# The first two chunks of z in another tile, TensorE's first waits filled; first expert tile's rows in the diagonal's tile, second list in smaller pieces

## Chip, cores and metric

One core of one Trainium2 chip. The metric is the device time of the whole kernel in microseconds (us); the kernel before has a median of 2366.27 us over 3 runs.

## What is computed

Eight batches of an attention without softmax, whose result is gated by u, and then a mixture of eight experts in which each token goes to its best one:

```python
scores = (1.0 / S) * np.matmul(z, z.transpose(0, 2, 1))      # z: 8 x 2496 x 64
out = np.matmul(np.maximum(scores, 0.0) ** 2, v)              # v: 8 x 2496 x 256
x = (u * out).reshape(B * S, D)                               # 19968 tokens of 256
logits = x @ w_gate                                           # 8 experts
expert_idx, gate_w = argmax(logits), softmax(logits) at that place
for e in range(8):                                            # w1: 256 x 1024, w2: 1024 x 256
    out[tokens of e] = gate_w * (np.maximum(x[tokens of e] @ w1[e], 0.0) @ w2[e])
```

All of it is fp32. TensorE gets each fp32 operand as two parts, a rounded high one and the low rest, and adds three products.

## The kernel before

**Attention.** A batch has five query chunks (four of 512, the last of 448) and ten pairs of key blocks for each: 400 steps in all, in the list `steps`. A step has `scores` (matmuls L292 and L293, ReLU and square on ScalarE, the high part L303 and the low part L305 on VectorE, or tiles that an earlier chunk has stored and that are turned back, L265 to L267) and `weighted` (matmuls L329 to L332 into the two `acc` banks). Scores are made three steps ahead (`LA`). The scores of a chunk with itself are kept in the tile `sd`, from which L298 mirrors one half.

**z and v.** `fetch_z` and `fetch_v` issue DMAs on SyncE's queue (SP), `split_z` (L117 to L123) and `split_v` (L133, L135) make the two parts. In the first batch the low part of v and the high part of the later z chunks are made on GpSimd (POOL). The tile `zr` has 2 buffers, `vr` 2.

**Routing.** After a chunk, `gate_x` makes x, `turn_rows` turns it into token rows by DMA transposes (L372), `logits` (L382 to L391) computes the logits and turns them into the tile `lg`, and `route` (choose from L420 on, exps, place) finds the expert and the place of each token, writes the rows to `xrows` in DRAM (L462, L464) and the token numbers to the list `lst` (L467). These pieces lie in a queue, `bg`, from which one is taken per step; `nothing` fills a turn.

**Experts.** `tile_list` makes a list of expert tiles. List "A" is made before the last batch ends and has six tiles of 512 tokens; list "F" needs all tokens and is made while list A's tiles run. A tile's rows are gathered (`load_x`, L681, 4 gathers on POOL into a tile `rows`, which has 3 buffers), turned (`turn_x`, L712, 4 DMA transposes on SP into `th`, of which there are 3), and the gate column is copied (L714, on VectorE, into `gt`); `split_x` (L724 to L727) makes the two parts of x. Then come 8 groups per tile: `up` (L744, 12 matmuls into a bank `ph`, L748 on ScalarE and L749 on VectorE) and `down` (L765, L767), two groups behind (`LU`). `ph` and `acc` share a ring of three PSUM banks. `finish` multiplies by the gate (L777) and scatters the rows out (L779). The weights of a tile are fetched by `load_w` (L672) and split by `split_piece` (L701 to L704).

**Order.** The Tile scheduler orders the instructions of each engine by a model of the time; each engine then runs its own in that order, and waits at the first that can't start. What is `pinned` is issued behind the last instruction so far of each engine. The table `loads` says at how many steps from the last one the first expert tile's weights and rows are fetched:

```python
    loads = {NKP + 4: [lambda: load_w(0, 0), lambda: load_w(0, 1)],
             NKP + 3: [lambda: load_x(0)],
             NKP - 1: [lambda: load_w(1, 0)],
             NKP - 4: [lambda: load_x(1)],
             NKP - 5: [lambda: turn_x(0)],
             1: [lambda: load_x(2)],
             0: [lambda: turn_x(1)]}
```

## Time and profile before

| | us |
|---|---|
| median of 3 runs (lowest, highest) | 2366.27 (2364.37, 2368.11) |
| the profiled execution | 2356.92 |
| its span | 2355.2 |
| TensorE busy | 2303.9 (98%) |
| VectorE busy | 1649.2 (70%) |
| ScalarE busy | 1423.5 (60%) |
| GpSimd busy | 641.6 (27%) |
| mean granted TensorE clock | 0.991 |

The span is what the trace covers; the profiled execution is 1.7 us longer and lies 9.35 us under the median. All times of the trace are counted from the span's start. The attention ends and the experts begin between 1365 and 1430 us; list A's tiles run first, the others follow to 2345 us.

### The profile page before, as it was taken

What the parts mean: (1) busy time and instruction counts of PE and PEld (TensorE: products, weight loads), DVE (VectorE), ACT (ScalarE), POOL (GpSimd) and SP (SyncE); (2) the same over time, 40 slices, a digit from 0 to 9 for tenths busy, and PEclk for the clock granted to TensorE, in tenths of its full rate; (3) what the DMA queues carried; (4) which work ended last, traced back from release to release, by engine and by line L of the source; (5) the groups of instructions that cost most, each with busy time, mean ns of one, the idle gap of its engine ahead of it and who ended that gap; (6) DMA issues with size and microseconds to landing.
All of it is one profiled execution on the core that took longest, in us unless ns stands there. A gap on an engine that the chain in (4) does not pass through costs nothing. (4 is left out here: it accounts for less than half of the span.)

```text
span 2355.2 us, 32513 instructions
## 1 busy us (share of the span) xinstructions
PE 2303.9 (98%) x11636; PEld 1937.7 (82%) x11636; DVE 1649.2 (70%) x3078; ACT 1423.5 (60%) x1944; POOL 641.6 (27%) x639
## 2 busy tenths in 40 slices
PE   8999999999999999999999988999999999999998
PEld 6888887888888888887888876788888888888887
DVE  8868868868868868868868846655666557557554
ACT  6757648658658648648658644355555556556443
POOL 4111111111111111111111225345445445346322
PEclk9999999999999999999999999999999999999999
DMA  5636637747647547547546767465657647557620
GB/s 136 102 65 120 114 62 121 109 68 133 103 69 139 88 78 135 91 74 131 98 75 115 126 114 130 115 150 166 170 140 193 148 133 198 149 147 190 148 87 28
DMA packets 424921, 280.16 MB, mean 119 GB/s; under 512 B 358380, under 2 KB 381690, under 8 KB 415536
## 3 DMA queue, kind: packets, MB, share of 16 engines
q1 hardware_dynamic: 393360, 158.91, 38.7%
q0 software_dynamic: 31392, 119.10, 18.5%
q8 instruction: 93, 1.52, 0.3%
q14 instruction: 76, 0.62, 0.1%
HBM read 149.79 MB, written 43.43 MB: 82 GB/s over the span
## 5 line engine op out<-in xcount | busy, mean ns | idle before, releaser
L332 PE MATMUL acc<-thi,t 128*128 128x512 f32 (+1 forms) x1600 | 619.9, 388 | 0.0
L329 PE MATMUL acc<-thi,t 128*128 128x512 f32 (+1 forms) x1600 | 595.7, 391 | 5.8 <-DVE thi L303 5.6
L331 PE MATMUL acc<-tlo,t 128*128 128x512 f32 (+1 forms) x1520 | 590.7, 389 | 4.3 <-DVE tlo L305 3.4
L765 PE MATMUL y<-t,t 128*128 128x512 f32 x1062 | 384.7, 399 | 4.5 <-ACT t L748 4.5
L749 DVE SCALAR_TENSOR_TENSOR t<-ph,t 128x512 fp32r<-128x512 f32 (+1 forms) x328 | 221.1, 675 | 235.0 <-ACT t L748 232.6
L744 PE MATMUL ph<-thi,t 128*128 128x512 f32 (+2 forms) x1248 | 379.9, 362 | 0.9 <-ACT thi L726 0.9
L467 POOL DMA_INDIRECT lst<-toks,posi x160 | 190.8, 1193 | 640.7 <-DVE posi L459 573.2
L748 ACT ACTIVATE t<-ph 128x512 fp32r<-128x512 f32 (+1 forms) x328 | 192.0, 588 | 279.6 <-PE ph L744 274.8
L329 PEld LDWEIGHTS acc<-thi,t 128*128 128x128 f32 x1600 | 300.9, 189 | 60.1 <-DVE thi L303 6.8
L332 PEld LDWEIGHTS acc<-thi,t 128*128 128x128 f32 x1600 | 301.8, 189 | 55.6
L331 PEld LDWEIGHTS acc<-tlo,t 128*128 128x128 f32 x1520 | 287.1, 189 | 58.7 <-DVE tlo L305 7.2
L767 PE MATMUL y<-t,t 128*128 128x256 f32 x1062 | 297.0, 283 | 10.8 <-DVE t L749 10.8
L744 PEld LDWEIGHTS ph<-thi,t 128*128 128x128 f32 x1248 | 227.3, 190 | 39.5 <-ACT thi L726 1.3
L765 PEld LDWEIGHTS y<-t,t 128*128 128x128 f32 x1062 | 200.8, 189 | 49.0 <-ACT t L748 4.9
L744 PE MATMUL ph<-tlo,t 128*128 128x512 f32 (+2 forms) x624 | 225.9, 362 | 0.8 <-DVE tlo L727 0.8
L767 PEld LDWEIGHTS y<-t,t 128*128 128x128 f32 x1062 | 202.3, 190 | 21.6 <-DVE t L749 12.6
L779 POOL DMA_INDIRECT out_dram<-tf,lfidx x136 | 143.3, 1054 | 276.5 <-DVE tf L777 246.6
L293 PE MATMUL ps_s<-t,t 128*128 128x512 f32 (+1 forms) x480 | 179.0, 377 | 0.0
L301 ACT ACTIVATE tf<-ps_s 128x1024 f32<-128x1024 f32 (+2 forms) x129 | 116.8, 906 | 92.2 <-PE ps_s L293 45.5
L681 POOL DMA_INDIRECT rows<-xrows,lfidx x136 | 141.3, 1039 | 44.1 <-issue 39.2
L303 DVE CAST thi<-tf 128x1024 fp32r<-128x1024 f32 (+2 forms) x129 | 85.1, 660 | 82.8 <-ACT tf L302 78.4
L267 DVE TENSOR_TENSOR tlo<-ps_s,thi 128x896 fp32r<-128x896 f32 (+1 forms) x80 | 89.1, 1114 | 61.4 <-ACT thi L266 60.9
(250 smaller groups left out, 3999.9 us busy)
## 6 DMA issues: line engine op xcount, KB each, us to landing
vr<-in_v_dram SPq DMA_DIRECT2D x80, 256.0 KB, 2.9
xrows<-rows SPq DMA_DIRECT2D x32, 544.0 KB, 3.9
u<-in_ut_dram SPq DMA_DIRECT2D x32, 512.0 KB, 4.5
zr<-in_zt_dram SPq DMA_DIRECT2D x40, 256.0 KB, 5.0
u<-in_ut_dram SPq DMA_DIRECT2D x8, 448.0 KB, 5.4
xrows<-rows SPq DMA_DIRECT2D x8, 408.0 KB, 3.6
rows<-th SPq DMA_TRANSPOSE x160, 4.7
lst<-toks,posi POOLq DMA_INDIRECT x160
```

The costliest lines, as they stand in the source:

```text
L293: nc.tensor.matmul(ps[:, i, m:n], lhsT=hl_k, rhs=lh_q[:, m:n], start=False, stop=True)
L329: nc.tensor.matmul(acc[d][:, :n], lhsT=vh, rhs=hi[:, i, :n], start=first and i == 0, stop=False)
L331: nc.tensor.matmul(acc[d][:, :n], lhsT=vh, rhs=lo[:, i, :n], start=False, stop=False)
L332: nc.tensor.matmul(acc[d][:, :n], lhsT=vl, rhs=hi[:, i, :n], start=False, stop=last and i == 1)
L467: i = nc.gpsimd.indirect_dma_start(out=lst1, out_offset=bass.IndirectOffsetOnAxis(ap=posi[:m, j:j + 1], axis=0), in_=toks[:m, col + j:col ...
L681: nc.gpsimd.indirect_dma_start(out=xg[:, s, :], out_offset=None, in_=src, in_offset=bass.IndirectOffsetOnAxis(ap=lists[which]["idx"][:, s, ...
L744: nc.tensor.matmul(o, lhsT=w1[:, part, dd, fs], rhs=xx[:, dd, :n], start=p == 0, stop=p == 5)
L748: nc.scalar.activation(hh[:, :m], ph[:, :m], AF.Relu)
L749: nc.vector.scalar_tensor_tensor(hl[:, :m], ph[:, :m], 0.0, hh[:, :m].bitcast(F32), op0=ALU.max, op1=ALU.subtract)
L765: nc.tensor.matmul(y, lhsT=hh[:, cs], rhs=w2[:, f % 2].rearrange("p i d -> p (i d)"), start=f == 0, stop=False)
L767: nc.tensor.matmul(y[:, 0:D], lhsT=hl[:, cs], rhs=w2[:, f % 2, 0, :], start=False, stop=f == NF - 1)
L779: d = nc.gpsimd.indirect_dma_start(out=out, out_offset=bass.IndirectOffsetOnAxis(ap=lists[which]["idx"][:, s, t:t + 1], axis=0), in_=yo[:, ...
```

## The change

At the start the first two chunks of z go into the tile `x` instead of the `zr` ring, so that the third one is fetched with them and each later one a step earlier; the low parts of the first two pieces of v are made on VectorE instead of GpSimd; and 4 and 8 warm-up matmuls on zeros are pinned behind the scores of step 0 and of step 1.

At the change from attention to experts the rows of the first expert tile are gathered into the tile `sd` (which gets the size of `rows`); `load_x`, `turn_x` and the gate copy (now `take_gates`, apart from `turn_x`) have new places in the table, and the functions in it are pinned. The last chunk's routing has four empty turns in `bg` instead of two. The second list is cut into 15 pieces instead of 9, and the weights of list F's first expert are fetched only after tile 3 has begun.

```diff
     def fetch_z(b, c):
         w = P * 4
-        zraw[b, c] = sb.tile([P, w], F32, name="zr", tag="zr", bufs=2)
+        if b == 0 and c < 2:
+            if c == 0:
+                zfirst.append(sb.tile([P, 2, QC], F32, name="x", tag="x"))
+            zraw[b, c] = zfirst[0][:, c]
+        else:
+            zraw[b, c] = sb.tile([P, w], F32, name="zr", tag="zr", bufs=2)
...
-        eng = nc.gpsimd if b == 0 else nc.vector
+        eng = nc.gpsimd if b == 0 and kp > 1 else nc.vector
...
+    fetch_z(0, 2)
     split_z(0, 0)
...
-        bg.extend([nothing] * 2 + route(b * S + q0, n, ns, lg, xr))
+        bg.extend([nothing] * (4 if b == B - 1 and c == NC_ - 1 else 2) + route(b * S + q0, n, ns, lg, xr))
...
-        return r, [count] + ([middle, others] if ns else []) + [experts, rows, nothing, nothing, lambda: places(0), lambda: places(1)]
+        return r, [count, middle, middle2, lambda: others([(0, nd, 2 * BS, ndbl)]),
+                   lambda: others([(1, nb, BS, nbig)]), remaining, lambda: experts(parts[:2]),
+                   lambda: experts(parts[2:]), experts2, rows, rows2, nothing, nothing,
+                   lambda: places(0), lambda: places(1)]
...
-        xg = ring_rows()
+        xg = ring_sd() if i == 0 else ring_rows()
...
-        gates[i] = sb.tile([P, BS], F32, name="gt", bufs=4)
-        nc.vector.tensor_copy(gates[i][:, 0:k], xgs.pop(i)[:, 0:k, D].bitcast(F32))
-        turned[i] = tp
+        turned[i] = tp
+
+    def take_gates(i):
+        gates[i] = sb.tile([P, BS], F32, name="gt", bufs=4)
+        nc.vector.tensor_copy(gates[i][:, 0:blocks[i]], xgs.pop(i)[:, 0:blocks[i], D].bitcast(F32))
...
+    pinned(lambda: warm_up(4))
     ready[1] = scores(*steps[1])
+    pinned(lambda: warm_up(8))
...
-             NKP + 3: [lambda: load_x(0)],
-             NKP - 1: [lambda: load_w(1, 0)],
-             NKP - 4: [lambda: load_x(1)],
-             NKP - 5: [lambda: turn_x(0)],
-             1: [lambda: load_x(2)],
-             0: [lambda: turn_x(1)]}
+             NKP + 2: [lambda: load_x(0)],
+             NKP + 1: [lambda: load_x(1)],
+             NKP - 1: [lambda: load_w(1, 0), lambda: turn_x(0)],
+             NKP - 3: [lambda: take_gates(0)],
+             NKP - 4: [lambda: load_x(2)],
+             NKP - 5: [lambda: turn_x(1)],
+             NKP - 7: [lambda: take_gates(1)]}
...
-            if kp % 2 == 0 and kp // 2 + 2 < NC_:
-                fetch_z(0, kp // 2 + 2)
+            if kp % 2 == 0 and kp // 2 + 3 < NC_:
+                fetch_z(0, kp // 2 + 3)
...
-                for w, h in ((wof[i] + 1, 1), (wof[i] + 2, 0)):
-                    if own[i] and w <= wof[hi - 1]:
+                for w, h in ((wof[i] + 1, 0), (wof[i] + 1, 1), (wof[i] + 2, 0)):
+                    if own[i] and w <= wof[hi - 1] and (w, h) not in weights and (w < NA or i > NA):
                         load_w(w, h)
...
             if i + 2 < hi and g == G // 2:
                 turn_x(i + 2)
+                take_gates(i + 2)
```

How the order of the instructions changes, at three places. VectorE at the start; L121 to L123 are the z split before (L130 to L132 now), L303 and L305 the parts of the scores (L318 and L320 now), L144 is the low part of v, L209 to L216 the constants:

```order
L121 CAST t_238<-zr 64x512
L123 TENSOR_TENSOR t_237<-zr,t_238 64x512
L121 CAST t_315<-zr 64x512
L303 CAST thi<-tf 128x1024
L122 TENSOR_TENSOR t_238<-zr,t_237 64x512
```

```order
L144 TENSOR_TENSOR t_196<-vr,t_196 128x512
L212 CAST e_down<-sd 128x8
L209 CAST wg_105<-wg_sb 128x2x8
...
L130 CAST t_251<-zr 64x512
L130 CAST t_328<-zr 64x512
L215 MEMSET x 1x272
L216 MEMSET x 128x256
L210 TENSOR_TENSOR wg_105<-wg_sb,wg_105 128x2x8
L131 TENSOR_TENSOR t_251<-zr,t_250 64x512
L213 COPY base<-base_121 128x8
L318 CAST thi<-tf 128x1024
```

The first high part of the scores now stands behind both low parts of v, most of the constants and a part of the splits of the third and fourth chunk of z.

VectorE at the end of attention; L714 is the gate copy before (L753 now), L267 the low part of a turned tile (L281 now), L702 and L704 weights (L738 and L740 now), L762 and L765 the split of x:

```order
L704 TENSOR_TENSOR t_13524<-s_13124,t_13524 128x2x256
L714 COPY gt<-rows 128x4
L702 TENSOR_TENSOR t_13552<-s_13124,t_13552 128x512
L267 TENSOR_TENSOR tlo<-ps_s,thi 128x2x448
L388 COPY lp<-lt 16x512
```

```order
L740 TENSOR_TENSOR t_13547<-s_13135,t_13547 128x2x256
L738 TENSOR_TENSOR t_13570<-s_13135,t_13570 128x512
L281 TENSOR_TENSOR tlo<-ps_s,thi 128x2x448
L753 COPY gt<-sd 128x4
L403 COPY lp<-lt 16x512
L404 COPY lp<-lt 16x512
L281 TENSOR_TENSOR tlo<-ps_s,thi 128x2x448
L383 COPY th<-x 128x1024
L740 TENSOR_TENSOR t_13571<-s_13135,t_13571 128x2x256
L762 COPY x<-th 128x1024
```

The gate copy now stands behind the low part on which the scores of the last chunk wait, and the split of the first expert tile three rows behind the next one.

SP from the rows of the fourth chunk on; L712 is `turn_x` before (L748 now), L391 the logits' transposes (L406 now), L372 the rows' (L387 now), L462 and L464 the writes of `xrows` (L477 and L479 now):

```order
L462 DMA xrows<-rows 128x4x272
L141 DMA u<-in_ut_dram 128x2x448
L712 DMA_TRANSPOSE th<-rows 128x4x128
L391 DMA_TRANSPOSE lg<-lp 128x4x16 x2
L372 DMA_TRANSPOSE rows<-th 128x4x128 x4
L712 DMA_TRANSPOSE th<-rows 128x4x128 x7
L462 DMA xrows<-rows 128x4x272
L712 DMA_TRANSPOSE th<-rows 128x4x128 x7
L391 DMA_TRANSPOSE lg<-lp 128x4x16 x2
L372 DMA_TRANSPOSE rows<-th 128x4x128 x4
L712 DMA_TRANSPOSE th<-rows 128x4x128
L462 DMA xrows<-rows 128x3x272
```

```order
L477 DMA xrows<-rows 128x4x272
L748 DMA_TRANSPOSE th<-sd 128x4x128 x4
L150 DMA u<-in_ut_dram 128x2x448
L406 DMA_TRANSPOSE lg<-lp 128x4x16 x2
L387 DMA_TRANSPOSE rows<-th 128x4x128 x4
L748 DMA_TRANSPOSE th<-rows 128x4x128 x4
L477 DMA xrows<-rows 128x4x272
L748 DMA_TRANSPOSE th<-rows 128x4x128 x5
L406 DMA_TRANSPOSE lg<-lp 128x4x16 x2
L387 DMA_TRANSPOSE rows<-th 128x4x128 x4
L748 DMA_TRANSPOSE th<-rows 128x4x128 x11
L477 DMA xrows<-rows 128x3x272
```

All four transposes of the first tile now come ahead of u and of the fourth chunk's logits. Ahead of the last chunk's logits stood 15 transposes of tiles 0 to 3, and stand 13 (tiles 0 to 2 and one of tile 3); the last chunk's rows come before the rest of tile 3.

## Rows read from the trace of the kernel before

**Rows 1.** The page: busy time of each engine, share of the span, instructions

```profile
PE 2303.9 (98%) x11636; PEld 1937.7 (82%) x11636; DVE 1649.2 (70%) x3078; ACT 1423.5 (60%) x1944; POOL 641.6 (27%) x639
```

**Rows 2.** Waits of TensorE, whole run: line, released by: us, times, longest

```profile
PE y L767 <- DVE t L749: 10.8, 4, 5.4
PE ps_s L292 <- DVE tlo L267: 6.9, 1, 6.9
PE acc L329 <- DVE thi L303: 5.6, 2, 4.5
PE y L765 <- ACT t L748: 4.5, 1, 4.5
PE acc L331 <- DVE tlo L305: 3.4, 3, 2.2
PE ps_s L292 <- DVE t L123: 2.3, 1, 2.3
```

**Rows 3.** Windows: stretch, us; busy of each engine; granted clock, DMA share, GB/s

```profile
0.00:40.00 40.00, 28.92 (x97) 20.22 (x98) 34.44 (x46) 28.63 (x33) 19.85 (x35) 0.87 0.61 168
1365.00:1430.00 65.00, 54.52 (x266) 46.02 (x265) 40.41 (x81) 26.14 (x38) 17.68 (x17) 0.89 0.65 135
1430.00:1550.00 120.00, 104.69 (x503) 86.00 (x503) 69.41 (x229) 50.60 (x84) 61.12 (x60) 0.95 0.66 138
1550.00:1700.00 150.00, 150.00 (x800) 128.74 (x799) 91.56 (x154) 84.68 (x147) 64.37 (x62) 1.00 0.56 150
```

**Rows 4.** Timeline of TensorE, 0 to 40 us

```profile
1.25 3.35 PE L149 MATMUL pw<-lp 128*128 128x512 bf16 x8 [1.25 <-DVE lp L146]
...
16.14 1.22 PE L329 MATMUL acc<-thi,t 128*128 128x512 f32 x2 [4.55 <-DVE thi L303]
```

**Rows 5.** Timeline of VectorE, 4 to 20 us: start, duration, line, operation, [idle before]

```profile
12.20 0.42 DVE L121 CAST t<-zr 64x512 fp32r<-64x512 f32 x1 [1.34 <-DMA zr<-in_zt_dram]
12.65 3.44 DVE L303 CAST thi<-tf 128x1024 fp32r<-128x1024 f32 x1
...
16.72 0.69 DVE L123 TENSOR_TENSOR t<-zr,t 64x512 fp32r<-64x512 f32 x1
...
18.58 0.69 DVE L303 CAST thi<-tf 128x1024 fp32r<-128x1024 f32 x1
```

**Rows 6.** Timeline of GpSimd, 2 to 40 us

```profile
12.22 0.86 POOL L118 CAST t<-zr 64x512 fp32r<-64x512 f32 x1 [2.38 <-DMA zr<-in_zt_dram]
13.05 2.48 POOL L135 TENSOR_TENSOR t<-vr,t 128x512 fp32r<-128x512 f32 x2
```

**Rows 7.** Timeline of VectorE, 1362 to 1430 us

```profile
1403.43 0.17 DVE L714 COPY gt<-rows 128x4 f32<-128x4 f32 x1 [12.83 <-DMA rows<-xrows,laidx]
```

**Rows 8.** Waits of VectorE, 1360 to 1552 us

```profile
DVE gt L714 <- DMA rows<-xrows,laidx: 32.3, 4, 12.8
DVE x L724 <- DMA th<-rows: 13.0, 4, 7.8
...
DVE lw L420 <- DMA lg<-lp: 7.0, 2, 6.5
```

**Rows 9.** Timeline of GpSimd, 1300 to 1470 us

```profile
1390.25 1.20 POOL L681 DMA_INDIRECT rows<-xrows,laidx  x1 [2.80 <-issue]
```

**Rows 10.** Timeline of TensorE, 1410 to 1556 us

```profile
1422.71 0.51 PE L744 MATMUL ph<-thi,t 128*128 128x512 f32 x1 [0.95 <-ACT thi L726]
```

**Rows 11.** Timeline of VectorE, 1430 to 1552 us

```profile
1453.49 0.21 DVE L420 COPY lw<-lg 128x64 uint16<-128x64 uint16 x1 [6.46 <-DMA lg<-lp]
...
1509.88 0.69 DVE L749 SCALAR_TENSOR_TENSOR t<-ph,t 128x512 fp32r<-128x512 f32 x1 [2.10 <-ACT t L748]
...
1521.46 0.33 DVE L636 CAST lfidx<-plt 128x52 int32<-128x52 f32 x2 [2.44 <-PE plt L634]
...
1546.23 0.75 DVE L724 COPY x<-th 128x1024 uint16<-128x1024 uint16 x1 [7.12 <-issue]
```

**Rows 12.** The page, DMA issues: out<-in, queue, count, KB, us to landing

```profile
xrows<-rows SPq DMA_DIRECT2D x32, 544.0 KB, 3.9
```

More of the change, by code (lines that the diff above doesn't have):

```diff
@@ L90, in ring_rows, with ring_sd @@
         return sb.tile([P, QC // P, ROW], I32, name="rows", tag="rows", bufs=3)
+    def ring_sd():
+        return sb.tile([P, QC // P, ROW], I32, name="sd", tag="sd")
     def ring_halves():
@@ L147, in fused_kernel, with warm_up @@
     ps = psm.tile([P, QC], F32, name="pw", tag="psm")
-    for i in range(8):
-        nc.tensor.matmul(ps, lhsT=warm[:, 0:P], rhs=warm, start=i == 0, stop=i == 7)
+    def warm_up(n):
+        for i in range(n):
+            nc.tensor.matmul(ps, lhsT=warm[:, 0:P], rhs=warm, start=i == 0, stop=i == n - 1)
+    warm_up(8)
     fetch_z(0, 0)
@@ L168, in fused_kernel @@
                             pattern=[[1, P]], channel_multiplier=-1)
-    raw = sb.tile([P, 2, QC], F32, name="sd", tag="sd").rearrange("p i n -> p (i n)").bitcast(I32)
+    raw = ring_sd().rearrange("p s r -> p (s r)")
     used = [0]
@@ L282, in scores @@
         elif late and kp % 2 == 0:
-            a = stored[b, c, c] = sb.tile([P, 2, QC], F32, name="sd", tag="sd")
+            sd = ring_sd().bitcast(F32).rearrange("p s r -> p (s r)")[:, 0:2 * QC]
+            a = stored[b, c, c] = sd.rearrange("p (i n) -> p i n", i=2)
         else:
@@ L540, in count @@
             nc.vector.scalar_tensor_tensor(units, done, -float(2 * BS), units, op0=ALU.mult, op1=ALU.add)
+        if ns:
+            want, ctake, take = t("want", (P, 2, E)), t("ctake", (P, 2 * E)), t("take", (P, 2, E))
         def middle():
-            want, ctake, take = t("want", (P, 2, E)), t("ctake", (P, 2 * E)), t("take", (P, 2, E))
             half = t("half")
@@ L556, in middle, with others @@
             nc.vector.scalar_tensor_tensor(units, take[:, 0, :], -3.0, units, op0=ALU.mult, op1=ALU.add)
-        def others():
-            full, nbig = t("full"), t("nbig")
-            for w, n, blocks_, number in ((0, nd, 2 * BS, ndbl), (1, nb, BS, nbig)):
+        def others(which):
+            for w, n, blocks_, number in which:
+                full = t("full")
                 floor_shift(full, units, blocks_.bit_length() - 1, "fi")
@@ L567, in others, with remaining @@
                                                op0=ALU.mult, op1=ALU.add)
+        def remaining():
             rem = t("rem")
@@ L581, in tile_list, with experts @@
                 parts.append((a, a + n, w))
-        def experts():
-            for a, z, w in parts:
+        def experts(some):
+            for a, z, w in some:
                 s3 = [P, z - a, E]
@@ L606, in rows, with rows2 @@
                                         op=ALU.mult)
+        def rows2():
             o = t("o", (P, NT))
@@ L636, in places, with all_of @@
                 nc.vector.tensor_copy(r["idx"][:, h * (SMALL // P) + s, 0:n], pt[:, s * NT:s * NT + n])
-        return r, [count] + ([middle, others] if ns else []) + [experts, rows, nothing, nothing, lambda: places(0), lambda: places(1)]
+        def all_of(*some):
+            return [lambda: [f() for f in some]]
+        if not ns:
+            return r, ([count] + all_of(lambda: experts(parts), experts2) + all_of(rows, rows2) + [nothing, nothing] +
+                       [lambda: places(0), lambda: places(1)])
+        nbig = t("nbig")
+        return r, [count, middle, middle2, lambda: others([(0, nd, 2 * BS, ndbl)]),
+                   lambda: others([(1, nb, BS, nbig)]), remaining, lambda: experts(parts[:2]),
+                   lambda: experts(parts[2:]), experts2, rows, rows2, nothing, nothing,
+                   lambda: places(0), lambda: places(1)]
     NF = F // P
@@ L912, in more @@
         turn_x(lo + 1)
+        take_gates(lo)
+        take_gates(lo + 1)
         split_x(lo)
```

6 lines of the change are left out of this document (5 added, 1 removed).

## Prediction

> **What bounds the kernel now.** I read the page first: TensorE is busy 2303.9 us, 98% of the span of 2355.2 [rows 1], so about 51 us are idle, and nothing that frees another engine is worth more than what it takes from those. Then the waits of TensorE [rows 2]: a few single waits make most of it, and nearly all end on VectorE. Then a table of windows [rows 3], which says where they lie and what the clock did: the start (0 to 40 us: 28.92 busy, clock 0.87), the end of attention up to the first expert tile (1365 to 1430: 54.52 busy, 0.89), and list A's tiles (1430 to 1550: 104.69 busy, 0.95). From 1550 to 1700 TensorE is busy in all 150 us at clock 1.00. The change works in the first three.
>
> Each stretch loses twice: the idle time, and the matmuls that run at the lower clock level (1.2 instead of 2.4 GHz) behind it. The second is bounded by (1 - clock) x length.
> - Start: 4.5 (of the 5.6 of L329, the other 1.1 lies at 1366) + 2.3 + 2.6 (of L331's 3.4) = 9.4 idle [rows 2]; clock at most 0.13 x 40 = 5.2 [rows 3], of which I count 4.3, as part of it falls on idle time. Together 13.7.
> - End of attention: 6.9 (L292) + 1.1 (the rest of L329) + 0.8 (the rest of L331) and smaller ones; in all the window shows 65 - 54.5 = 10.5 idle. Clock at most 0.11 x 65 = 7.2, some 2.5 of it in the idle time, so 4.6. Together 15.1.
> - List A's tiles: 10.8 (L767) + 4.5 (L765) = 15.3 [rows 2]; clock 0.05 x 120 = 6.0. Together 21.3.
>
> **Part 1, the start.** Removed: TensorE stood 4.55 us until 16.14 [rows 4] for the first high part of the scores, a cast that took 3.44 us at 12.65 where the same one took 0.69 at 18.58 [rows 5]. In between POOL ran a cast until 13.08 and two low parts of v until 15.53 [rows 6]: VectorE's cast ended about when POOL did. Moved: two of POOL's four low parts of v go to VectorE, ahead of that cast (2 x about 0.7), with constants (some ten small ones, 0.17 each as the copy in [rows 7], to 0.2) and a part of the splits of z's third and fourth chunk (two casts of 0.42 and one of the parts of 0.69 [rows 5]). The second chunk of z has landed at about 6.0 in both kernels; its three instructions and the low parts of v end near 8.8 on VectorE, the rest of the queue ahead of the cast takes 10 x 0.2 + 2 x 0.42 + 0.69 = 3.5, so the cast starts at about 12.4 and ends at 13.1 if POOL is silent. The first accumulation starts there instead of 16.14: 2.9 us. If the wait of 2.3 for z's second chunk shrinks too it is hidden in this, since the next wait ends later. With a shorter wait that has warm-ups in it, half speed behind 16 us (2.6 of the 4.3) goes; of the later wait and its clock (2.6 idle, 1.7 clock) I take 1.0. Sum 2.9 + 2.6 + 1.0 = 6.5. Ends: 3, if the cast is still held; 10, if the later waits go too.
>
> Added: 12 warm-ups of 0.42 (8 in 3.35 at the start [rows 4]), at full clock about half, 2.7 together; 4 of them stand inside the scores of step 0 and delay the first ReLU by 0.9, which is before VectorE's queue reaches the cast. I cost them at nothing; without cover 2.7.
>
> By the Trainium skill (GPSIMD Engine Reference, "Key points") POOL and VectorE contend when VectorE's instruction has two SBUF inputs or runs in a two-port mode. The trace agrees for a cast [rows 5, 6]; the low part of v moved to VectorE has two such inputs, so by this rule it only moves the contention, and the start would give 3 and not 6.5.
>
> **Part 2, the end of attention.** VectorE waited 32.3 us in four gate copies [rows 8], of them 12.83 until 1403.43 [rows 7]: a copy of 0.17 that waits for the rows of the second half of tile 0, gathered late because all three buffers of `rows` are taken. Behind it stood the low part L267, and behind that the scores of the last chunk: L292's 6.9. Now tile 0 is gathered into `sd`, which is free when L298 has read it (1365), on POOL 8 gathers of 1.2 [rows 9] for tiles 0 and 1, so issued by about 1375, well ahead of 1403; SP turns tile 0 ahead of the last u. The copy stands behind L267 and has its data some 20 us before. So 6.9 goes, and the clock's 2.6 behind it; the copy ahead of the low parts at 1365 is gone (1.1 + 0.8); tile 0's transposes are not the last thing before 1422.71 [rows 10] any more (0.95 and the rest of the idle 10.5, and 1.7 of the clock). I take all 15.1, less 0.3 for rounding: 14.8. Low end 9.5: the big wait alone. Added: SP's u and the fourth chunk's logits wait for tile 0's gathers; u is needed when the last accumulation ends, some 20 us later, so nothing.
>
> **Part 3, list A's tiles.** Four places. (a) lw, 6.46 until 1453.49 [rows 11], and behind it 5.4, L767's longest [rows 2]; (b) the split of F's second tile, 7.12 until 1546.23 [rows 11], and (c) the gate copy of tile 3, one of the four in [rows 8], which share the other 5.4 of L767 (3.7 and 1.7 by where they lie); (d) a split of x that waited 7.8 [rows 8], and L765's 4.5. All are one kind: VectorE stands at the head of its queue for a DMA, behind it waits the low part of h (L749), of which one is wanted every 2.79 us (0.69 + 2.10 idle at 1509.88 [rows 11]).
> What is late next, in the new order:
> - The gate of tile 3 stands behind the fifth L749 instead of the fourth; its chain from the fourth chunk's reciprocal at about 1415 (write 3.9 [rows 12], four gathers of 1.2 [rows 9], a landing that I put at that of the write) ends at about 1428 to 1429, its need is at about 1430: 0 to 1.3.
> - lw stands behind the eighth instead of the sixth, 2 x 2.79 us of room, and the logits' transposes go out some 9 us earlier because TensorE is 12 us earlier: nothing.
> - Tile 3's split waits for transposes that still stand behind the last chunk's rows on SP: about 1.6, and 2 at the next PSUM bank; tiles 4 and 5 0 to 0.5.
> - F's second and third tile are split behind the same L749 (the 37th) now. The first list of places came 24.8 us before that split (1521.46 to 1546.23 [rows 11]) and comes about 26.6 before the need now, but the third tile's split stands between: 0 to 4.7, with clock.
> Sum of what stays: 4 to 10 with the clock that goes with it; I take 9 of the 21.3, so 12.3 come back. Low end 4 (most waits only change their names), high end 17. List F's 15 pieces hold the same instructions, on VectorE, which idles half of the stretch: nothing.
>
> **Sum.** 6.5 + 14.8 + 12.3 = 33.6. Against the profiled execution of 2356.9 that is 2323.3; the median lies 9.35 above that execution, and I take the same offset: 2366.3 - 33.6 = 2332.7, so **2332.5**. The forecast's own range is 2324 to 2340.
>
> **The rivals.** Bounds of 0.2% (4.7 us) separate faster and slower from no change.
> - *The waits only move* (0.24). For it: each DMA that VectorE waited for still comes, and three of them stay on SP's queue behind the last chunk's logits and rows; and the stretch of these waits had a clock of 0.95 [rows 3]. Then part 3 gives 4, part 2 about 11, part 1 about 4: 19, so 2347. Against it: 12.8 us of the 32 in gate copies [rows 7, 8] and the copy at 1365 fall away by the order alone.
> - *The start stays held by POOL* (0.12). POOL keeps two low parts of v, two casts of z and its seven DMAs for the constants. If the first cast again ends with POOL, part 1 gives 3 at most and perhaps takes 1: 2336 to 2340. Inside the forecast's range nearly; it changes the explanation more than the time.
> - *Everything in list A's stretch fits* (0.10): part 3 gives 19, the start 8: 2366 - 42 = 2324.
> - *The start or the end of attention is not as the order says* (0.05): the model that orders the instructions expects other durations, and part 2's split of tile 0 stands on VectorE 5 us ahead of transposes that are late; only one part in three comes: 2350 to 2361.
> - *List F comes too late* (0.04), the slower side. The list in 15 pieces ends behind the 32nd up instead of between the 30th and 31st; its gathers, transposes and split take 25 us, 9 ups, so the first tile is ready behind the 41st, and list A's tiles end with the 48th. From 7 turns of delay on, every further turn costs 2.79. To eat 33.6 and 4.7 more it would have to be (38.3 / 2.79) = 14 turns beyond those 7. Just possible if `bg`'s last pieces wait for the last chunk's places: 2372 and more.
>
> By the Trainium skill (TensorE: Matmul & The Clock Gate, "What's actually happening") the array is throttled by default and activity releases it; that rule gives the warm-ups the clock's 2.6 of part 1. No row here shows a warm-up inside a wait.
>
> **How the numbers follow.** Forecast 0.45, the rivals as given. 2320 to 2350 holds the forecast, the held start, the case in which everything fits, and most of the moved waits, some 0.82. Faster by over 0.2%: 0.91; within it 0.05 (the weak end of the fourth rival, and half of the unknown); slower 0.04.
>
> **What would show it.** In the new profile the waits of TensorE should sum to about 20 instead of 41 us. Start: first L329 row near 13, its cast at 0.7, no half clock behind 16. End of attention: no wait at L292 for the low part of a turned tile, a gate copy without idle time ahead of it, the first `ph` matmul near 1404 (1422.71 less 6.5, less 12). List A: lw without idle time, at most 4 us at splits of x, one wait near F's second tile. It is wrong if VectorE shows waits of 5 us and more at lw, at gate copies or at the split of x in that stretch, if the first cast still takes 3 us, or if TensorE waits between 1550 and 1700 where it never did.

## The result, and the profile after

The changed kernel takes 2333.36 us (median of 4 runs, 2330.92 to 2335.68) where the kernel before takes 2365.32 on the same chip (2361.71 to 2368.11): a ratio of 0.9878 with a 95% interval of 0.9855 to 0.9902, 23 to 34 us less. The forecast was 2332.5.

Its profiled execution took 2330.92 us, 26.0 less than that of before (2356.92), with a span of 2329.2. I follow those 26.0 us through the trace; why the medians lie 32 apart comes further down. The page, then the waits of TensorE over the whole run (line, releaser: us, times, longest), then the same four windows as before:

```profile
PE 2300.1 (99%) x11648; PEld 1933.9 (83%) x11648; DVE 1648.3 (71%) x3080; ACT 1425.7 (61%) x1944; POOL 642.9 (28%) x637
```

```profile
PE ph L782 <- DVE t L787: 4.7, 2, 4.1
PE acc L346 <- DVE tlo L320: 3.3, 3, 2.3
PE acc L346 <- DVE tlo L324: 2.3, 3, 0.9
PE ps_s L307 <- ACT sd L316: 2.0, 3, 0.9
PE acc L344 <- DVE thi L318: 1.5, 2, 1.3
PE y L805 <- DVE t L787: 1.4, 1, 1.4
```

```profile
0.00:40.00 40.00, 33.61 (x128) 23.02 (x129) 35.70 (x51) 29.24 (x33) 18.02 (x33) 0.96 0.69 174
1365.00:1430.00 65.00, 64.63 (x349) 55.55 (x348) 43.18 (x90) 34.92 (x48) 29.13 (x31) 1.00 0.91 167
1430.00:1550.00 120.00, 112.94 (x535) 93.06 (x534) 73.85 (x230) 53.85 (x91) 61.31 (x59) 0.93 0.57 142
1550.00:1700.00 150.00, 150.00 (x801) 128.72 (x801) 89.91 (x152) 82.75 (x146) 65.33 (x63) 1.00 0.58 154
```

Idle time between matmuls fell from 41.3 us to 19.2. Against [rows 2, 3]: the wait of the last chunk's scores (6.9) is gone, and in the end of attention TensorE is busy 64.63 of 65 us at clock 1.00, where it was 54.52 at 0.89. In the start it is busy 33.61 of 40 instead of 28.92, at 0.96 instead of 0.87. List A's stretch has 7.1 us of idle time instead of 15.3, but its clock is lower than before, 0.93 instead of 0.95.

A second measure is used from here on, the **lead**: how much earlier a given matmul starts than the same one (counted along its line) in the profile of before. It adds up what was won until there, idle time and clock together.

| matmul (its start before) | lead, us |
|---|---|
| 152nd of the 1520 accumulations L346, L331 before (160.0) | 4.24 |
| 1368th of them (1274.9) | 0.99 |
| first down matmul on 256 columns, L805, L767 before: the first `y` below (1430.2) | 16.56 |
| 103rd of these (1520.7) | 24.43 |
| last of these (2345.1) | 26.03 |

**The start.** Timelines of TensorE, of VectorE and of GpSimd, 0 to 40 us (start, duration, line, operation, [idle before <- releaser]):

```profile
13.07 0.73 PE L344 MATMUL acc<-thi,t 128*128 128x512 f32 x2 [1.34 <-DVE thi L318]
...
17.30 0.49 PE L346 MATMUL acc<-tlo,t 128*128 128x512 f32 x1 [2.25 <-DVE tlo L320]
...
18.00 0.63 PE L346 MATMUL acc<-tlo,t 128*128 128x512 f32 x1
```

```profile
12.34 0.68 DVE L318 CAST thi<-tf 128x1024 fp32r<-128x1024 f32 x1
...
14.37 1.74 DVE L131 TENSOR_TENSOR t<-zr,t 64x512 fp32r<-64x512 f32 x1
16.04 1.21 DVE L320 TENSOR_TENSOR tlo<-tf,thi 128x1024 fp32r<-128x1024 f32 x1
17.17 3.47 DVE L318 CAST thi<-tf 128x1024 fp32r<-128x1024 f32 x2
```

```profile
15.79 4.30 POOL L144 TENSOR_TENSOR t<-vr,t 128x512 fp32r<-128x512 f32 x2
```

The first cast starts at 12.34 and takes 0.68 where it took 3.44 [rows 5], and the first accumulation starts at 13.07 instead of 16.14 [rows 4]. But POOL's next two low parts of v start at 15.79, behind the DMAs for the constants, where two stood at 13.05 [rows 6], and what they now stand beside is the low part L320, which takes its usual 1.21, and the next two casts, which are held: 3.47 for two that take about 0.7 each alone. TensorE waits 2.25 for L320, and the matmuls from 17.6 to 21.1 take 0.63 instead of 0.40: half clock behind the wait. L320 itself was not held but late: between the first cast and it stand three pieces of z's split (13.04 to 16.11), the last of which took 1.74 where 0.68 is usual.

**The end of attention.** Timelines of VectorE and of TensorE:

```profile
1390.77 0.16 DVE L753 COPY gt<-sd 128x4 f32<-128x4 f32 x1
...
1403.05 0.16 DVE L753 COPY gt<-rows 128x4 f32<-128x4 f32 x1
```

```profile
1408.16 0.39 PE L782 MATMUL ph<-thi,t 128*128 128x512 f32 x1
```

Both gate copies stand without idle time where one had 12.83 us [rows 7], and the first expert matmul starts at 1408.16, 14.55 earlier than at 1422.71 [rows 10].

**List A's tiles.** Waits of VectorE from 1360 to 1552 us; then SP's timeline, and VectorE's and TensorE's behind it:

```profile
DVE x L762 <- DMA th<-rows: 14.7, 4, 7.4
...
DVE gt L753 <- DMA rows<-xrows,laidx: 4.9, 1, 4.9
DVE gt L753 <- DMA rows<-xrows,lfidx: 4.1, 1, 4.1
```

```profile
1426.60 7.31 SPq L387 DMA_TRANSPOSE rows<-th  x4
1434.01 11.87 SPq L748 DMA_TRANSPOSE th<-rows  x8
```

```profile
1441.02 0.75 DVE L762 COPY x<-th 128x1024 uint16<-128x1024 uint16 x1 [7.38 <-DMA th<-rows]
```

```profile
1442.38 0.79 PE L782 MATMUL ph<-thi,t 128*128 128x512 f32 x1 [4.13 <-DVE t L787]
```

Gate copies cost VectorE 9.0 us instead of 33.8 (32.3 [rows 8] and 1.5 in list F), and `lw` 1.3 instead of 7.0 [rows 8]. The split of x has not gone: 14.7 instead of 20.1 (13.0 [rows 8] and the 7.12 marked as issue [rows 11]). The longest is that of tile 3. Its transposes stand on SP's queue behind the last chunk's rows, which take 7.31 us; VectorE's wait ends at 1441, and TensorE waits 4.13 and then 0.56. In the trace its matmuls run at half clock from 1441.1 to 1451.3 behind that. The other wait that stayed is near list F's second tile: 0.94 and 1.43 at 1528 to 1530, with half clock from 1529.8 to 1536.6. The two stretches together explain the 0.93 of the window.

### The profile page after: what moved, and what is told of

It is laid out like the page before. It is cut to its first block, busy times and chain, and to the rows that moved or that the text cites. A ratio compares the mean times of both kernels' runs of the same rounds, so it can differ in the third digit from the quotient of the medians.

```text
span 2329.2 us, 32537 instructions
## 1 busy us (share of the span) xinstructions
PE 2300.1 (99%) x11648; PEld 1933.9 (83%) x11648; DVE 1648.3 (71%) x3080; ACT 1425.7 (61%) x1944; POOL 642.9 (28%) x637
## 4 chain that ended last, share of the span: by engine, by line
PE 90%; DMA 3%; DVE 2%; issue 2%; ACT 1%; SPq 1%; POOL 0%; POOLq 0%; ACTq 0%; DVEq 0%
PE ph L782 17%; PE acc L347 14%; PE acc L344 14%; PE acc L346 14%; PE y L803 12%; PE y L805 6%; PE ps_s L307 4%; PE ps_s L308 4%; PE ps_s L279 3%; DMA vr<-in_v_dram 1%; PE pt L394 1%; DMA th<-rows 1%; PE ps_s L313 1%; DMA lg<-lp 1%; DMA rows<-xrows,lfidx 0%
## 5 line engine op out<-in xcount | busy, mean ns | idle before, releaser
L346 PE MATMUL acc<-tlo,t 128*128 128x512 f32 (+1 forms) x1520 | 589.2, 388 | 5.6 <-DVE tlo L320 3.3
L786 ACT ACTIVATE t<-ph 128x512 fp32r<-128x512 f32 (+1 forms) x328 | 192.3, 588 | 284.8 <-PE ph L782 274.7
L346 PEld LDWEIGHTS acc<-tlo,t 128*128 128x128 f32 x1520 | 286.1, 188 | 59.8 <-DVE tlo L320 6.5
L805 PE MATMUL y<-t,t 128*128 128x256 f32 x1062 | 295.8, 281 | 1.4 <-DVE t L787 1.4
L805 PEld LDWEIGHTS y<-t,t 128*128 128x128 f32 x1062 | 201.4, 190 | 11.6 <-DVE t L787 2.3
L316 ACT ACTIVATE tf<-ps_s 128x1024 f32<-128x1024 f32 (+2 forms) x129 | 117.0, 907 | 69.6 <-DVE tlo L315 34.9
L318 DVE CAST thi<-tf 128x1024 fp32r<-128x1024 f32 (+2 forms) x129 | 84.3, 654 | 82.9 <-ACT tf L317 78.3
L281 DVE TENSOR_TENSOR tlo<-ps_s,thi 128x896 fp32r<-128x896 f32 (+1 forms) x80 | 89.2, 1115 | 65.3 <-ACT thi L280 64.5
```

What stands on the lines that cost most here:

```text
L346: nc.tensor.matmul(acc[d][:, :n], lhsT=vh, rhs=lo[:, i, :n], start=False, stop=False)
L786: nc.scalar.activation(hh[:, :m], ph[:, :m], AF.Relu)
L805: nc.tensor.matmul(y[:, 0:D], lhsT=hl[:, cs], rhs=w2[:, f % 2, 0, :], start=False, stop=f == NF - 1)
```

## The experiments

The kernels ran on four chips, each beside runs of the kernel before on the same chip: the first four of the table, after_again, the next four, and the last two. Leads are against the profile of before that the prediction used; a second trace of the unchanged kernel (before_again, one execution of 2352.49 us beside after_again) leads it by 2.6 at 1275 us, 6.5 at the first `y`, 5.7 at the 103rd and 4.5 at the end, so a lead means little below some 4 us.

| run | median | before there | ratio, 95% | lead: first `y` | 103rd `y` | last |
|---|---|---|---|---|---|---|
| start_only | 2362.55 | 2364.81 | 0.9969 to 1.0000 | 4.8 | 4.8 | -8.1 |
| trans_only | 2353.70 | 2364.81 | 0.9938 to 0.9973 | 18.2 | 27.2 | 3.9 |
| no_sd | 2353.27 | 2364.81 | 0.9918 to 0.9968 | 18.9 | 29.5 | -1.4 |
| gates_with_turn | 2351.35 | 2364.81 | 0.9917 to 0.9961 | 19.9 | 27.9 | 4.2 |
| after_again | 2325.99 | 2361.46 | 0.9817 to 0.9884 | 22.3 | 30.4 | 30.8 |
| table_only | 2347.43 | 2358.60 | 0.9932 to 0.9966 | 14.4 | 15.9 | 7.2 |
| gates_late_only | 2354.43 | 2358.60 | 0.9963 to 0.9996 | 10.3 | 14.0 | 6.9 |
| nothing2 | 2341.26 | 2358.60 | 0.9907 to 0.9945 | 20.8 | 24.4 | 19.2 |
| rows_late_v | 2336.80 | 2358.60 | 0.9867 to 0.9939 | 21.5 | 31.0 | 18.5 |
| trans_only_again | 2363.33 | 2379.51 | 0.9885 to 0.9948 | 16.5 | 21.3 | -6.2 |
| after_third | 2363.69 | 2379.51 | 0.9891 to 0.9951 | 9.8 | 16.3 | -6.7 |

### The start alone, and the rest alone

start_only is the kernel before with the change's lines for the start, and trans_only is the change without them (the later fetches of z go with them):

```diff
+        if b == 0 and c < 2:
+            if c == 0:
+                zfirst.append(sb.tile([P, 2, QC], F32, name="x", tag="x"))
+            zraw[b, c] = zfirst[0][:, c]
...
-        eng = nc.gpsimd if b == 0 else nc.vector
+        eng = nc.gpsimd if b == 0 and kp > 1 else nc.vector
...
+    pinned(lambda: warm_up(4))
...
+    pinned(lambda: warm_up(8))
```

> Kernel before with the change's start alone (first two z chunks in the tile x, third chunk fetched at once, two low parts of v on VectorE, 12 warm-ups). Theory (the parts add up, the start is worth what the trace of the change shows at 160 us): TensorE is 4 us ahead at 160 us, time 2361 (2357 to 2364), first accumulation at 13.1, half clock once for 3.4 us near 18, and the end of attention as before, its 6.9 us wait at L292's place included. Rival (the start gives nothing that lasts, as the trace of the change is only 0.9 us ahead from 580 us on): 2365, and the lead is gone by 600 us here too.

> The change without its start part. Theory: first accumulation at 16.1 as before, and all of the 15.6 us at the end of attention and the 7.4 us in list A's tiles: 2365 - 23 = 2342 (2337 to 2346). Rival (the two parts are not independent, the earlier start changes when DMAs collide later): 2333 as the whole change, or above 2350.

start_only, timelines of TensorE and of VectorE:

```profile
13.19 0.73 PE L340 MATMUL acc<-thi,t 128*128 128x512 f32 x2 [1.43 <-DVE thi L314]
...
17.41 0.79 PE L342 MATMUL acc<-tlo,t 128*128 128x512 f32 x1 [1.75 <-DVE tlo L316]
```

```profile
17.29 3.45 DVE L314 CAST thi<-tf 128x1024 fp32r<-128x1024 f32 x2
```

The first accumulation, the held second pair of casts and the lead at 160 us (4.16) are those of the whole change, so the lead there comes from this part alone. Half clock lasts from 14.5 to 21.3, longer than expected, and the wait of the last chunk's scores is 4.6 instead of 6.9. How much the start is worth in the first 160 us is less sure than one trace says. Of the six traces with the old start, the profile of before and gates_late_only lie at 0 and -0.2 at 160 us and run at half clock a second time, from 34.9 and 35.4 us on; the other four do not, and lie at 1.6. The seven with the change's start lie between 3.7 and 4.4. So it is worth between 2.1 and 4.6 us there, and 2.8 between the two traces of the second pair (after_again and before_again). In the time of the whole kernel it is 2.3 us, with an interval that ends at no change. trans_only has the end of attention without the start (a lead of 18.2 at the first `y`, 1.7 of it from the first 160 us), and still gains only 11 us: its trace loses 14 us between the 103rd `y` and 1560 us and 9 more later. Those losses were on no list of mine. Waits of TensorE in trans_only, 1500 to 1560 us:

```profile
PE y L797 <- issue: 8.1, 3, 6.1
PE y L799 <- issue: 2.9, 2, 1.6
```

### Which part frees the last chunk's scores

Two theories: tile 0 in `sd` frees the buffers of `rows`, so tile 1 comes earlier; or the gate copies apart from the transposes stand where nobody waits behind them. One kernel takes back each, and two more make the kernel before with one of them alone: table_only moves `load_x` and `turn_x` (with the copies inside), gates_late_only moves the copies and nothing else.

```diff
     no_sd, against the change:
-        xg = ring_sd() if i == 0 else ring_rows()
+        xg = ring_rows()
...
     gates_with_turn, against the change:
-             NKP - 1: [lambda: load_w(1, 0), lambda: turn_x(0)],
-             NKP - 3: [lambda: take_gates(0)],
+             NKP - 1: [lambda: load_w(1, 0), lambda: turn_x(0), lambda: take_gates(0)],
...
-             NKP - 5: [lambda: turn_x(1)],
-             NKP - 7: [lambda: take_gates(1)]}
+             NKP - 5: [lambda: turn_x(1), lambda: take_gates(1)]}
...
     table_only, against the kernel before:
-             NKP + 3: [lambda: load_x(0)],
-             NKP - 1: [lambda: load_w(1, 0)],
-             NKP - 4: [lambda: load_x(1)],
-             NKP - 5: [lambda: turn_x(0)],
-             1: [lambda: load_x(2)],
-             0: [lambda: turn_x(1)]}
+             NKP + 2: [lambda: load_x(0)],
+             NKP + 1: [lambda: load_x(1)],
+             NKP - 1: [lambda: load_w(1, 0), lambda: turn_x(0)],
+             NKP - 4: [lambda: load_x(2)],
+             NKP - 5: [lambda: turn_x(1)]}
...
     gates_late_only, against the kernel before:
+             NKP - 7: [lambda: pinned(lambda: take_gates(0))],
...
+             0: [lambda: turn_x(1), lambda: pinned(lambda: take_gates(1))]}
```

> The change, but tile 0's rows are gathered into the ring rows as before; the gate copies keep their late places. In the order two of tile 0's gathers go early, and tile 2's wait for a buffer that the gate copy of tile 0 sets free (near 1398), so that they land near 1408. Theory A (the place of the gate copy behind L281 was what counted): the 6.9 us wait stays away, VectorE stands 3 to 4 us for tile 2's gate, 2333 + 3 = 2336. Theory B (the tile sd was what counted): a wait of 5 us or more before the last chunk's scores and half clock behind it, 2343 or more.

> The change, but the gate copies of tiles 0 and 1 are made with their transposes, 2 and 2 steps earlier, tile 0 in sd. Theory A (gathered early, the copy never waits wherever it stands): 2333, within 3. Theory B (the place of the copy was what counted): VectorE waits at the copy of tile 0 or 1 for 5 us or more, 2340 or more.

> The kernel before with nothing but the new places of load_x and turn_x in the table (tile 1's rows are gathered some 25 us earlier), the gate copies inside turn_x and the ring rows as before. Theory now (the wait of 12.8 us belongs to tile 1's copy, and what counts is when tile 1's rows are gathered; neither sd nor the copy's place): no wait of 5 us at the last chunk's scores, first ph matmul 14 to 16 us earlier than before, list A's tiles with the waits at lw and at F's second tile as before; in all 15 us less than before. Rival (the copy's late place or sd is needed too): 5 us or more of wait left at the last chunk's scores, less than 9 us gained.

> The kernel before with nothing but the gate copies taken out of turn_x and pinned later; all gathers at their old times. Theory (a late place is the second way to the same end): the wait of 6.9 us at the last chunk's scores goes too, tile 0's split still stands at its late transposes (about 2 us), 8 to 11 us less than before at the first ph matmul. Rival (the copy's place does nothing as long as the rows come late, the wait moves to the split of x): under 4 us at the first ph matmul.

The 6.9 us wait is gone in all four (0.8 is left in gates_with_turn), so neither the tile `sd` nor the separate copies are needed for it; an earlier gather of tile 1 does it, and so does a later copy. What differs is what becomes late next. no_sd (VectorE):

```profile
1402.52 0.17 DVE L753 COPY gt<-rows 128x4 f32<-128x4 f32 x1 [3.89 <-DMA rows<-xrows,laidx]
```

table_only (VectorE, then TensorE):

```profile
1403.25 0.17 DVE L714 COPY gt<-rows 128x4 f32<-128x4 f32 x1 [5.29 <-DMA rows<-xrows,laidx]
```

```profile
1404.60 0.67 PE L329 MATMUL acc<-thi,t 128*128 128x448 f32 x2 [2.92 <-DVE thi L303]
```

gates_late_only (VectorE, then TensorE):

```profile
1408.51 0.75 DVE L727 COPY x<-th 128x1024 uint16<-128x1024 uint16 x1 [4.98 <-DMA th<-rows]
```

```profile
1411.84 0.80 PE L747 MATMUL ph<-thi,t 128*128 128x512 f32 x1 [5.30 <-ACT thi L729]
```

Without `sd` it is the third tile's copy that comes late, now that three tiles share the three buffers of `rows`: VectorE waits 3.89, TensorE 1.44 and 1.11 behind the end of attention. With the table alone the same copy holds the last accumulations for 2.92. With the copies alone the transposes of tile 0 come as late as before, and the first `ph` waits 5.30 for its split. So each part takes away what another leaves. From 1275 us to the first `y` the whole gains 15.6 (16.2 and 12.2 in its other two traces), the table alone 11.2, the copies alone 7.5 by the leads, and 3.9 is what the unchanged kernel's second trace shows there by itself. Without `sd` it is 13.1 and with the copies at the transposes 14.0: inside the change's own spread, so neither of these two is shown to be worth anything by itself. Behind the first `y` the table alone gains 1.5 up to the 103rd, the whole change 7.9: the difference is in the parts that table_only lacks, the empty turns and list F in pieces among them.

### What decides list A's tiles

nothing2 takes back two of the empty places ahead of the last chunk's routing. rows_late_v keeps the change, lets tile 3's transposes go ahead of the last chunk's rows on SP, and gives two more low parts of v to VectorE:

```diff
     nothing2, against the change:
-        bg.extend([nothing] * (4 if b == B - 1 and c == NC_ - 1 else 2) + route(b * S + q0, n, ns, lg, xr))
+        bg.extend([nothing] * 2 + route(b * S + q0, n, ns, lg, xr))
...
     rows_late_v, against the change:
-        eng = nc.gpsimd if b == 0 and kp > 1 else nc.vector
+        eng = nc.gpsimd if b == 0 and kp > 3 else nc.vector
...
+        if late_rows:
+            bg.extend([nothing] * 4 + [lambda: sends.pop()()] + [nothing] * 0)
...
+            if gi == 5:
+                turn_x(3)
```

> The change with two empty turns for the last chunk instead of four; lw stands behind the sixth L787 in the order instead of the eighth. Theory (lw needs the room): VectorE stands 3 to 6 us at lw, TensorE 2 to 5 and half clock behind it: 4 to 8 us more than the change, with the wait at the split of tile 3 smaller, as both wait for the same queue. Rival (the logits come early enough since TensorE is earlier): as the change within 2 us.

> The change, with the last chunk's row transposes sent behind tile 3's, and the low parts of the first four pieces of v on VectorE. Theory (tile 3's split waits for its transposes behind those rows, and POOL's low parts of v hold VectorE's second cast): the wait of 4.1 us near 1440 and its clock go (4 to 8 us), the wait of 2.25 near 17 and its clock go (2 to 4): 6 to 10 us less than the change, 29 to 45 less than before. Rival (the list's last rows come later by as much and F's first tiles wait for them; VectorE's own queue at the start gets longer): the waits only move, within 3 us of the change.

nothing2, timelines of SP and of TensorE:

```profile
1427.97 1.21 SPq L748 DMA_TRANSPOSE th<-rows  x1
1433.37 0.36 SPq L477 DMA_DIRECT2D xrows<-rows  x1
...
1434.39 7.80 SPq L748 DMA_TRANSPOSE th<-rows  x6
```

```profile
1446.10 0.80 PE L782 MATMUL ph<-thi,t 128*128 128x512 f32 x1 [9.66 <-DVE t L787]
```

rows_late_v, timelines of SP, of TensorE (a wait at the start, then the largest from 1424 to 1450 us) and of VectorE at the start:

```profile
1419.30 2.48 SPq L413 DMA_TRANSPOSE lg<-lp  x2
1421.88 5.03 SPq L759 DMA_TRANSPOSE th<-rows  x3
1427.19 5.15 SPq L390 DMA_TRANSPOSE rows<-th  x4
```

```profile
16.74 0.50 PE L346 MATMUL acc<-tlo,t 128*128 128x512 f32 x1 [1.81 <-DVE tlo L320]
...
1429.37 0.48 PE L793 MATMUL ph<-thi,t 128*128 128x512 f32 x1 [0.61 <-issue]
...
1432.84 0.80 PE L814 MATMUL y<-t,t 128*128 128x512 f32 x1 [0.99 <-ACT t L797]
```

```profile
20.01 3.46 DVE L320 TENSOR_TENSOR tlo<-tf,thi 128x1024 fp32r<-128x1024 f32 x2
```

With two places less, the last chunk's writes to `xrows` come between the transposes of tile 3; they wait for their data until 1433.37, SP stands behind them from 1429.2 on, and TensorE waits 9.66 instead of 4.13. From the first to the 103rd `y` nothing2 gains 3.6 where the change gains 7.9. The loss of 4.3 is what was expected, but not its reason: `lw` has no wait there, and the wait at tile 3's split became longer, not smaller. With tile 3's transposes ahead of the rows the wait of 4.13 is gone; 0.6 to 1.0 stay in its place, with half clock from 1431.8 to 1438.7. So SP's order there sets what tile 3's split costs. It gave back less than the 4 to 8 us expected: from the first to the 103rd `y` rows_late_v gains 9.5, the change 7.9, 8.1 and 6.5 in its three traces. The start of rows_late_v has a lead of 5.29 at 160 us and no half clock at all, but no_sd, whose start is the change's, has none there either. POOL's hold has moved once more, to the low parts at 20.01, and the wait for L320 near 17, which was to go with POOL's low parts of v, is still 1.81. Its 31.0 at the 103rd `y` is only 0.6 over after_again's 30.4, and it did not run beside the change, so it is not shown to be faster.

### The same kernel on other chips

> The changed kernel once more, unchanged, beside runs of the kernel before on the same chip as the four experiments. Theory (the four experiments lost their time to waits that lie in them, 11 to 14 us of gain where 23 to 32 were expected): 2333 as before, with no unexplained waits of VectorE and ScalarE behind 1500 us. Rival (those waits come with the chip or the execution, not with the edit): waits marked as issue behind 1500 us here too, and a time of 2345 to 2352.

> The kernel before once more, unchanged, for a second trace. Theory: 2365, and its list F part behind 1560 us without a wait over 2 us, as in its first trace. Rival (the waits behind 1500 us come with the execution): several of them here too, and the same time only because something else was shorter.

Beside each other on one chip the change takes 2325.99 and the kernel before 2361.46, 35 us apart; their traces lie 26.3 apart at the last `y` matmul (30.8 less 4.5), as in the first pair. Waits of TensorE in after_again from 1430 to 1560 us are those of the change's first trace, and there are no others over 0.5 behind 1530:

```profile
PE ph L782 <- DVE t L787: 4.8, 2, 4.2
PE y L805 <- DVE t L787: 2.4, 1, 2.4
PE y L803 <- ACT t L786: 2.1, 1, 2.1
```

The kernels on the other two chips had lost 5 to 31 us of lead behind the 103rd `y`, where the change lost none in either trace. Either that belonged to their orders of instructions, or to the chips; the last two runs put the change and one of those kernels on a further chip.

> The kernel of the run trans_only, unchanged. In that run's trace TensorE had waits between 1500 and 1970 us, some 23 us in all, beside which the trace shows no releaser, and which neither the kernel before nor the change had in their own traces. If they belong to this order of instructions, they are here again at the same rows, TensorE's lead over the kernel before falls by 15 us or more between the first y and 1560 us, and the time is about 11 us under the kernel before. If they belong to the one execution or its chip, they are gone or elsewhere here, and the time is 20 to 25 us under the kernel before, near 24.4 us of lists and the end of attention together less the 3 to 5 us of the start.

> The change itself once more, beside the run trans_only_again on the same chip. If the waits without a releaser belong to the order of instructions, the change has none over 3 us behind 1530 us, as in its two traces, and is some 20 us faster than trans_only_again. If they belong to the chip or the execution, it has them here as trans_only_again has, or neither has, and the two lie 4 to 10 us apart: the start alone (4.2 us in the traces), and what the second piece of list E, F's later transposes and the smaller pieces do.

The two take the same time, 2363.3 and 2363.7, and the change loses there as the others do. Timelines of after_third, TensorE and ScalarE:

```profile
1524.44 0.40 PE L782 MATMUL ph<-thi,t 128*128 128x512 f32 x1
1532.18 0.77 PE L803 MATMUL y<-t,t 128*128 128x512 f32 x1 [7.34 <-issue]
...
1534.66 0.41 PE L805 MATMUL y<-t,t 128*128 128x256 f32 x1
1540.96 1.22 PE L803 MATMUL y<-t,t 128*128 128x512 f32 x2 [5.89 <-ACT t L786]
```

```profile
1529.93 0.47 ACT L814 ACTIVATE tf<-y,gt 128x256 f32<-128x256 f32 x1 [4.44 <-remote]
...
1530.81 0.84 ACT L814 ACTIVATE tf<-y,gt 128x256 f32<-128x256 f32 x2
1540.31 1.58 ACT L786 ACTIVATE t<-ph 128x512 fp32r<-128x512 f32 x3 [8.66 <-remote]
```

"issue" and "remote" say that the profile names no releaser. The three ReLUs L786 from 1540.31 on need `ph` banks whose matmuls had ended at 1521.59, 1523.13 and 1524.84 by their records, and ScalarE was free from 1531.65; it starts 8.66 us later all the same, and TensorE stands 5.89 for it. (In the change's first trace they started at 1514.21, 1514.91 and 1516.27, at most 0.7 us behind their `ph`.) What ScalarE waited for came late: the semaphore by which TensorE releases it is recorded as raised at 1529.91 and then not until 1540.29. Whether TensorE's work or only its signal was late can't be told, as the ten traces of these three chips are not whole: they hold 6 to 7% fewer updates of the semaphores of TensorE, VectorE and ScalarE than the recorded instructions make, most of them missing behind 1300 us, while the four traces of the first and the second pair hold all within 0.1%. So "issue" and "remote" can stand there for a releaser that was not recorded. Whether the recording itself costs time on these chips was not tried. The instructions of ScalarE, VectorE and POOL stand in the same order in all three traces of the change, so the stall is no matter of the order. Of TensorE's idle time behind 1500 us, summed over its rows without the end, the first pair has 5.2 before and 2.4 after, the second 5.4 and 4.4, after_third 18.7, and the kernels on the other two chips 9.9 to 24.6, start_only (14.0) among them, whose order there is nearly that of the kernel before. The losses come with the chip, or the execution, and hit mostly what runs from 1500 us on; no trace of the kernel before was taken on these three chips. So a time on one chip is to be held only against the kernel before on the same chip, and even the gain depends on where the change runs: 32.0, 35.5 and 15.8 us.

## Why the prediction was right, point by point

The time came out within a microsecond of 2332.5; the sum behind it was too large, and another assumption covered that.

- **The offset.** Step that failed: "the median lies 9.35 above that execution, and I take the same offset". After's profiled execution lies only 2.4 under its median, so of the medians' 32.0 only 26.0 are in the traces, 7.6 less than the 33.6 forecast. That the median came out right is in this measure luck: a profiled execution can lie anywhere among the runs, and the change's own effect is known no closer than the spread of executions and chips.
- **Part 1, forecast 6.5, measured 4.2 at 160 us.** The path of the first cast held: forecast 12.4, came at 12.34 (0.68 long, first accumulation at 13.07). The step that failed is "with a shorter wait ... half speed behind 16 us ... goes": a second wait came, 2.25 for the low part L320, and half clock at 17.7 behind it. The sum had no term for it. L320 stood on VectorE behind three pieces of z's split, and in rows_late_v, where POOL has no low part of v before 20.63, 1.81 of it is left. POOL's low parts of v moved to 15.79 with the constants' DMAs and held the second pair of casts; this is the rival "the start stays held by POOL", one cast later than it was put, but what TensorE waits behind it is only 0.61. By the Trainium skill (GPSIMD Engine Reference, "Key points") POOL and VectorE contend when VectorE's instruction has two SBUF inputs or runs in a two-port mode. The prediction read a start of 3 from that, and with the 2.1 to 4.6 of all traces this lies nearer than 6.5, though more than half of the longest wait came from VectorE's own queue. The traces agree for low parts, which have two inputs (3.46 for a pair in rows_late_v), and show the same on casts (3.47 for a pair). Of the 4.2, 1.0 was left at 1275 us in this trace, 6.0 and -2.4 in the other two of the change: waits of 0.3 to 1.6 us near 360, 537 and 1060 us, which traces of both kernels have, come out differently from one execution to the next. Whether the new start makes them longer stays open. The warm-ups were not tried by themselves. With the same ones half clock starts at 17.7 and 18.3 in two traces of the change and at 14.5 in the third, so what they do for the clock is not shown.
- **Part 2, forecast 14.8, measured 15.6** (the lead from 1275 us to the first `y`; 12.4 between the second pair of traces). The gate copy, the split of tile 0 and the clock behind them went as written. One reading was wrong: the copy at 1403.43 [rows 7] is that of tile 1, not of "the second half of tile 0". What its lateness hangs on, a buffer of `rows` that comes free too late, fits the trace of before: POOL stood until 1389.43 for the write `xrows<-rows` issued at 1380.18, and only then gathered tile 1. `sd` was shown not to be needed against it. The first `ph`, forecast near 1404, came at 1408.16: of the start, 5.5 less was left by then than I had counted.
- **Part 3, forecast 12.3, measured 7.9** (first to 103rd `y`). The mechanism was right, the size off: "Tile 3's split waits ... about 1.6, and 2 at the next PSUM bank" was 4.13 and 0.56, with ten microseconds at half clock behind it, at most 5 us more. I had priced the rows ahead of these transposes too low: they held SP's queue for 7.31. The wait near F's second tile was 2.4, with 6.8 us at half clock behind it, so up to 5.8 where 0 to 4.7 with clock was written. By the prediction's own sign, a wait of VectorE of 5 us and more at the split of x (7.38), this part was wrong. Together 13.4 of the 21.3 stayed, not 9. How the missing 4.4 divides is not shown: without tile 3's wait rows_late_v gains only 1.4 to 3.0 more than the change. The gate of tile 3 (4.9 on VectorE, more than the 0 to 1.3 written, but nothing on TensorE) and `lw` (1.3) cost TensorE nothing, as written.
- **The rest.** No wait appeared between 1550 and 1700 us; the 15 pieces of list F and the warm-ups cost nothing that the trace shows; 2.05 of the last lead came between 1811 and 1901 us, 1.5 of it from a wait for VectorE at 1884 that the trace of before has there and the change has not.
- **The rivals.** "The waits only move" is what the partial kernels show: the table alone moved the wait to the third tile's copy, the copies alone moved it to tile 0's split, and two empty places less doubled the one at tile 3's. Together they leave only that last one. List F did not come too late: in the change's trace TensorE waits for nothing of its first tile, and VectorE 2.34 at its split. ScalarE came to the split of F's second tile 24 to 25 us behind the list's first gather in the change's first two traces, and 30.8 in after_third; there it did not wait for rows but stood behind the stall of 8.66. No rival of mine had the chip in it.

## What to carry to other kernels

When a queue stands for a late DMA, ask for each part of the cure what becomes late next: here two different edits removed the same 6.9 us wait, and each alone gave back 3 to 5 us one step further on. Read the queue that issues the DMAs as carefully as the engine that waits: behind four transposes in front of the wanted ones TensorE stood 4 us and ran ten at half clock, of which another order gave back 1.4 to 3.0 by the leads, within their spread. A forecast made against one profiled execution needs that execution's place among the runs as a term with bounds of its own, and a few per mille of gain need the kernel before on the same chip.

## What the runs showed of the hardware that was not expected

- On three of the chips ScalarE, and VectorE beside it, stood 4 to 11 us at a time though the matmuls that they wait for had ended by their records: 4.44 and 8.66 in after_third, 10.64 in trans_only_again. ScalarE has 2 to 8 stalls over 4 us without a named releaser behind 1430 us in every trace of these chips. The change's traces on the first and the second pair's chip have none there on either engine; those of the kernel before have them only at the split of x, which waits for transposes. An 8 KB instruction fetch ended 0.4 us ahead of the one at 1540.31, but none lies near the one at 1529.93, and most others have none either. The late semaphore and the missing records are said above: the cause stays open.
- A kernel's median moves from chip to chip by more than what was to be measured: 2358.6 to 2379.5 for the unchanged kernel, 2326.0 to 2363.7 for the change.
- A VectorE operation can take several times as long beside POOL's tensor operations: a cast of 0.68 took 3.44 in the kernel before, a pair of them 3.47 in the change, a pair of low parts 3.46 in rows_late_v. Not each does: the low part at 16.04 in the change took 1.21, as elsewhere, and POOL's own two 4.30 instead of 2.48.
